# Attention and a routed expert layer on one core: a smaller first warming tile, and one store for both row halves at the end

## The chip, the cores and the metric

The kernel runs on one core of one Trainium2 chip. Its metric is the device time of one execution in microseconds; lower is better. The kernel before takes 374.43 us (median of three runs, 373.29 to 374.58). A profile of one execution, taken by the hardware, shows what each engine of the core did: TensorE (PE; its weight loads PEld), VectorE (DVE), ScalarE (ACT), GpSimd (POOL) and SyncE (SP), and the 16 DMA engines.

## The reference

The kernel computes grouped-query attention and then a two-level routed expert layer on its output. Cut to what matters:

```python
# q: (8, 16, 384, 64), k and v: (8, 4, 384, 64), all float32; four query heads share one k and v
scores = (1 / sqrt(64)) * q @ k.T
attn = softmax(scores)
x = (attn @ v).transpose(0, 2, 1, 3).reshape(8 * 384, 1024)

g_idx = argmax(x @ w_group)            # 4 groups, softmax weight g_w of the chosen one
e_idx = argmax(x_of_group @ w_expert)  # 4 experts in the group, softmax weight e_w
h = maximum(x_of_expert @ w1[g, e], 0)         # 1024 -> 1024
out[tokens] = g_w * e_w * (h @ w2[g, e])       # 1024 -> 1024, out: (3072, 1024) float32
```

The kernel works batch by batch. It guesses one expert for each batch of 384 tokens, computes that expert for all tokens of the batch, and weights the rows. What a guess leaves over is done in a loop at the end, which runs zero times for these inputs.

## The kernel before

Two places matter: the first eight microseconds and the last fifteen. `P` is 128, `S` 384, `SC` 3 (chunks of 128 tokens in a batch), `NC` 6, `DM` 1024, `HALF` 512, `FQ` 8, `B` 8.

At the start, TensorE multiplies a tile of ones, so that it is busy while the first keys and queries arrive:

```python
onesb = cpool.tile([P, 4 * P], BF16)
nc.vector.memset(onesb, 1.0)
nc.sync.dma_start(out=k0f[:, 0], in_=rows(k[0])[:, 0])
for m in range(KG):
    nc.scalar.dma_start(out=q0f[:, m], in_=rows(q[0])[:, m])
# ... (cut: the other loads; on ScalarE's queue also the gate weights, 8 and 32 rows)

def first_k(gp, which, eng):      # keys of the first two kv heads, transposed
    lo = gp * NC
    pt = ps_tile(which, [P, 16, P], BF16)
    for i in range(NC):
        for s in range(2):
            nc.tensor.transpose(out=pt[s * D:(s + 1) * D, i, :], in_=k16[0][:, lo + i],
                                identity=id128b)
    evac(eng, kT[0][:, lo:lo + NC, :], pt[:, :NC, :])   # copy to SBUF on eng

def first_scores():
    # ... (cut)
    def fill(n):                  # n warming products of 512 columns
        for i in range(n):
            nc.tensor.matmul(out=warm[:, i % 2, :], lhsT=onesb[:, :P], rhs=onesb, start=True,
                             stop=True)

    fill(8)
    nc.vector.tensor_copy(out=k16[0][:, :NC].rearrange("p c d -> p (c d)"), in_=k0f[:, 0])
    nc.scalar.copy(out=qraw[0][:, 0], in_=q0f[:, 0])
    nc.vector.tensor_copy(out=qraw[0][:, 1], in_=q0f[:, 1])
    first_k(0, "s", nc.vector)
    fill(2)
    first_q(0, SC, "s", nc.scalar)      # first query head pair, transposed, copied by ScalarE
    first_q(SC, SC, "o", nc.vector)     # second
    fill(2)
    return fill
# ... (cut) then the first two score tiles, and fill(4)
```

`k0f` and `q0f` are float32 as loaded; the three copies cast them to bfloat16.

At the end, the last batch's second product is done chunk by chunk, in halves of 512 columns. Each half is scaled by the row weight `w` on its way from PSUM to SBUF and stored at once. A chunk's 128 partitions are two groups of 64, which belong to different row sets of the output: row `6 * p + x` for partition `p` of the group, with `x` = 0 and 2 for chunk 0, 4 and 1 for chunk 1, 3 and 5 for chunk 2.

```python
def out_rows(o):
    return o.rearrange("(p x) d -> x p d", x=NC)

def halves(c):
    for h in range(2):
        j = 2 * c + h
        yield slice(h * H2, (h + 1) * H2), 2 * (j % SC) + j // SC

for c in range(SC):
    ot = opool.tile([P, DM], F32, name="ot")
    for nh in range(2):
        y = ps_tile("so"[nh])
        ffn_y(w2s[B - 1], hTs[B - 1], c, "", (nh,), y)      # eight products of 512 columns
        sl = slice(nh * HALF, (nh + 1) * HALF)
        w = weff[B - 1][:, c:c + 1]
        if (c, nh) == (SC - 1, 1):
            q1 = slice(HALF, HALF + HALF // 2)
            q2 = slice(HALF + HALF // 2, DM)
            nc.scalar.mul(ot[:, q1], y[:, nh, :HALF // 2], w)
            nc.vector.tensor_scalar(ot[:, q2], y[:, nh, HALF // 2:], w, None, op0=ALU.mult)
        elif nh:
            nc.vector.tensor_scalar(ot[:, sl], y[:, nh, :], w, None, op0=ALU.mult)
        else:
            nc.scalar.mul(ot[:, sl], y[:, nh, :], w)
        for i, (ps, x) in enumerate(halves(c)):
            eng = nc.scalar if (c, nh, i) == (SC - 1, 1, 1) else nc.sync
            eng.dma_start(out=out_rows(out[(B - 1) * S:])[x][:, sl], in_=ot[ps, sl])
```

Of the kernel before, what the change touches and what calls it, by code (L numbers as in the profile page):

```python
# [10 lines left out]
BF16 = mybir.dt.bfloat16  # L11
I32 = mybir.dt.int32
AX = mybir.AxisListType
ALU = mybir.AluOpType
# [4 lines left out]
def kernel(  # L19
# [11 lines left out]
    nc = tc.nc  # L31
    P = 128
    B, Hq, S, D = q.shape
    _, Hkv, _, _ = k.shape
    SC = S // P
    DM = Hq * D
# [5 lines left out]
    FQ = F // P  # L42
    NW = G + NE
    HALF = DM // 2
# [10 lines left out]
    cpool = ctx.enter_context(tc.tile_pool(name="const", bufs=1))  # L55
# [15 lines left out]
    def ps_tile(which, shape=None, dtype=F32):  # L71
        if which == "x":
            which = f"o{1 - turn['o']}"
        else:
            turn[which] = 1 - turn[which]
            which += str(turn[which])
        return psum.tile(shape or [P, 2, 512], dtype, name="ps_" + which)
# [6 lines left out]
    def rows(x):  # L84
        return x.rearrange("h (p c) d -> (h p) (c d)", c=NC).rearrange("(a p) n -> p a n", p=P)
# [19 lines left out]
    def new_qT(b):  # L105
        qT[b] = xpool.tile([P, KQ * SC, P], BF16, name="qT")

    def new_kT(b):
        kT[b] = xpool.tile([P, NK, P], BF16, name="kT")
# [36 lines left out]
                              in_=v[0, g0:g1].rearrange("h (p c) d -> p h (c d)", c=NC))  # L146

    onesb = cpool.tile([P, 4 * P], BF16)
    nc.vector.memset(onesb, 1.0)
    nc.sync.dma_start(out=k0f[:, 0], in_=rows(k[0])[:, 0])  # L150
    for m in range(KG):
# [10 lines left out]
    for g in range(1, Hkv):  # L162
        nc.gpsimd.dma_start(out=qraw[0][:, KG * g:KG * (g + 1)],
                            in_=rows(q[0])[:, KG * g:KG * (g + 1)])
# [73 lines left out]
    def evac(eng, out_, in_):  # L238
        if eng is nc.scalar:
            eng.copy(out=out_, in_=in_)  # L240
        else:
            eng.tensor_copy(out=out_, in_=in_)  # L242

    def first_k(gp, which, eng):
# [6 lines that stand above are left out]
        evac(eng, kT[0][:, lo:lo + NC, :], pt[:, :NC, :])  # L251

    def first_q(i0, n, which, eng):
        pt = ps_tile(which, [P, 16, P], BF16)
        for i in range(n):
            a, c = (i0 + i) // SC, (i0 + i) % SC
            nc.tensor.transpose(out=pt[:, i, :], in_=qraw[0][:, a, c * P:(c + 1) * P],
                                identity=id128b)
        evac(eng, qT[0][:, i0:i0 + n, :], pt[:, :n, :])

    def first_scores():
        new_kT(0)
        new_qT(0)
        warm = ps_tile("o")

        def fill(n):
            for i in range(n):
                nc.tensor.matmul(out=warm[:, i % 2, :], lhsT=onesb[:, :P], rhs=onesb, start=True,  # L268
                                 stop=True)

        fill(8)
        nc.vector.tensor_copy(out=k16[0][:, :NC].rearrange("p c d -> p (c d)"), in_=k0f[:, 0])
        nc.scalar.copy(out=qraw[0][:, 0], in_=q0f[:, 0])
        nc.vector.tensor_copy(out=qraw[0][:, 1], in_=q0f[:, 1])
        first_k(0, "s", nc.vector)
        fill(2)
        first_q(0, SC, "s", nc.scalar)
        first_q(SC, SC, "o", nc.vector)
        fill(2)
        return fill  # L280
# [263 lines left out]
    weff = {}  # L544
# [13 lines left out]
    ers, w1s, w2s = {}, {}, {}  # L558
# [39 lines left out]
# [8 lines that stand above are left out]
# [11 lines left out]
    def ffn_y(w2, hT, c, which, nhs=(0, 1), y=None, fs=None):  # L617
        if y is None:
            y = ps_tile(which)
        for nh in nhs:  # L620
            for f in (range(FQ) if fs is None else fs):
                nc.tensor.matmul(out=y[:, nh, :], lhsT=hT[:, f, c * P:(c + 1) * P],  # L622
                                 rhs=w2[:, f, nh * HALF:(nh + 1) * HALF],
                                 start=(f == 0), stop=(f == FQ - 1))
        return y
# [10 lines left out]
    hTs = {}  # L636
# [23 lines left out]

    gate_constants()
    fill = first_scores()
    index_constants()
    at = {0: Attn(0), 1: Attn(1)}
# [215 lines left out]

    for c in range(SC):
        ot = opool.tile([P, DM], F32, name="ot")
        for nh in range(2):
            y = ps_tile("so"[nh])
            ffn_y(w2s[B - 1], hTs[B - 1], c, "", (nh,), y)
            sl = slice(nh * HALF, (nh + 1) * HALF)
            w = weff[B - 1][:, c:c + 1]
            if (c, nh) == (SC - 1, 1):
                q1 = slice(HALF, HALF + HALF // 2)
                q2 = slice(HALF + HALF // 2, DM)  # L890
                nc.scalar.mul(ot[:, q1], y[:, nh, :HALF // 2], w)
                nc.vector.tensor_scalar(ot[:, q2], y[:, nh, HALF // 2:], w, None, op0=ALU.mult)
            elif nh:
                nc.vector.tensor_scalar(ot[:, sl], y[:, nh, :], w, None, op0=ALU.mult)
            else:
                nc.scalar.mul(ot[:, sl], y[:, nh, :], w)
            for i, (ps, x) in enumerate(halves(c)):
                eng = nc.scalar if (c, nh, i) == (SC - 1, 1, 1) else nc.sync
                eng.dma_start(out=out_rows(out[(B - 1) * S:])[x][:, sl], in_=ot[ps, sl])
    region.close()  # L900

    n_left = nc.values_load(left_i[0:1, 0:1], min_val=0, max_val=B * NE)
# [1 line left out]
    with tc.For_i(0, n_left, 1):  # L904
# [15 lines left out]
        x = xpool.tile([P, KQ, S], BF16, name="xb")  # L920
# [15 lines left out]
        for c in range(SC):  # L936
            ot = opool.tile([P, DM], F32, name="ot")
            for ps, x_ in halves(c):
                nc.sync.dma_start(out=ot[ps], in_=orows[x_])
            y = ffn_y(w2, hT, c, "s")  # L940
            nc.vector.scalar_tensor_tensor(ot, y.rearrange("p a n -> p (a n)"), we[:, c:c + 1],
                                           ot, op0=ALU.mult, op1=ALU.add)
# [32 lines left out]
```

The softmax here doesn't subtract the row's maximum and nothing guards it: scores larger than these inputs give would overflow.

## Time and profile before

| | before |
|---|---|
| time, median of three runs | 374.43 us |
| span of the profiled execution | 372.4 us |
| TensorE clock granted, mean | 0.994 |
| first warming product starts | 1.60 us |
| first key transposes start | 5.13 us |
| first scores start | 7.52 us |
| last output products start | 363.75 us |
| last stores are issued | 366.70 us |
| stores in the last chunks | 12 of 128 KB each |

The profile's times are microseconds from the start of the span. A line of the timeline has the start, the duration, the engine, the line of the kernel, the operation, the tiles (written <- read) and the number of instructions merged into it. What stands in brackets is the idle time of the engine just before, and what ended it. An engine's name with a `q` is its queue, which issues DMAs and waits; the duration of an issue is that of issuing and not of the transfer. The DMA view gives packets, megabytes and the time that the packets took as a share of 16 engines' time, by queue: q1 is SyncE's, q10 ScalarE's, q0 GpSimd's. Under its issues stand the size and the median time from issue to landing.

### The profile page before, as it was taken

The page shows a single profiled execution, that of the slowest core. Times are in us where ns is not written, and L with a number is a line of the kernel's source. Part 1 is how long each engine was busy: PE and PEld are TensorE (multiplying, and loading weights), DVE is VectorE, ACT ScalarE, POOL GpSimd, SP SyncE. Part 2 cuts the span into 40 slices and gives each one's busy share as a digit, 9 for nine tenths or more (in the row PEclk, how much of TensorE's full clock was granted, in tenths as well). Part 3 has the DMA queues.
Part 4 walks back from the last instruction along what each step waited for, and adds up shares of the span by engine and source line. Part 5 has one row for each costly group of instructions (what it writes and reads, how often), then busy time and mean ns, then how long its engine had stood idle before and what let it go on. Part 6 is the DMA issues. An engine that isn't in the chain of part 4 may idle for free.

```text
span 372.4 us, 8914 instructions
## 1 busy us (share of the span) xinstructions
PE 361.1 (97%) x3648; PEld 183.8 (49%) x3663; DVE 258.1 (69%) x491; ACT 233.0 (63%) x309; POOL 150.6 (40%) x118
## 2 busy tenths in 40 slices
PE   8999999999999999999999999999999999999992
PEld 3545446445454545544555445544545445554641
DVE  5699787858976498737989189764897379892230
ACT  4789943759926597367954599265972679544221
POOL 6666950706804176033730367113760237500000
PEclk9999999999999999999999999999999999999997
DMA  8986999999999999999999999989999999999734
GB/s 189 242 108 101 241 213 156 234 239 281 222 152 184 249 263 210 147 195 291 238 208 153 255 246 216 199 167 246 264 212 150 203 212 238 196 201 234 238 73 99
DMA packets 71209, 76.02 MB, mean 204 GB/s; under 512 B 35928, under 2 KB 50264, under 8 KB 71168
## 3 DMA queue, kind: packets, MB, share of 16 engines
q0 software_dynamic: 26640, 41.03, 63.0%
q1 hardware_dynamic: 44096, 33.81, 37.1%
q8 instruction: 29, 0.48, 0.5%
q10 hardware_dynamic: 432, 0.61, 0.5%
q14 instruction: 12, 0.10, 0.1%
HBM read 89.21 MB, written 18.87 MB: 290 GB/s over the span
## 4 chain that ended last, share of the span: by engine, by line
PE 91%; DVE 3%; ACT 2%; issue 1%; POOL 1%; ACTq 0%; POOLq 0%
PE ps_o L324 29%; PE ps_s L611 21%; PE ps_s L622 14%; PE ps_s L305 8%; PE ps_o L622 8%; PE ps_o L446 3%; PE ps_o L268 2%; DVE red L338 1%; PE ps_o L611 1%; PE ps_o L408 1%; ACT e L311 1%; PE ps_s L473 1%; DVE ps_o L419 1%; DVE xT L428 1%; POOL e L331 1%
## 5 line engine op out<-in xcount | busy, mean ns | idle before, releaser
L311 ACT ACTIVATE e<-ps_s 128x768 f32<-128x768 f32 x192 | 150.3, 814 | 22.1 <-PE ps_s L305 19.3
L324 PE MATMUL ps_o<-e,v_raw 64*64 64x384 f32 x1536 | 153.1, 482 | 0.2 <-DVE xT L428 0.2
L331 POOL TENSOR_TENSOR e<-e 128x768 f32<-128x768 f32 x64 | 116.1, 1832 | 88.6 <-ACT e L311 64.6
L338 DVE TRANSPOSE_TENSOR_REDUCE red<-e 128x24 f32<-128x768 f32 x128 | 114.3, 947 | 11.9 <-POOL e L331 11.9
L611 PE MATMUL ps_s<-xb,w 128*128 128x384 bf16 x480 | 81.1, 326 | 0.4 <-ACT hT L615 0.2
L324 PEld LDWEIGHTS ps_o<-e,v_raw 64*64 64x64 f32 x1536 | 55.4, 133 | 37.5 <-issue 27.1
L611 PEld LDWEIGHTS <-w 128*128 128x128 bf16 x512 | 48.9, 98 | 36.1 <-issue 3.9
L305 PE MATMUL ps_s<-qT,kT 64*64 64x384 bf16 x768 | 63.7, 326 | 0.4 <-ACT e L311 0.2
L615 ACT ACTIVATE hT<-ps_s 128x768 bf16<-128x768 f32 x30 | 24.3, 810 | 61.0 <-PE ps_s L611 61.0
L622 PEld LDWEIGHTS <-hT 128*128 128x128 bf16 x384 | 35.5, 98 | 45.1 <-issue 6.5
L622 PE MATMUL ps_s<-w,hT 128*128 128x512 bf16 x240 | 56.0, 379 | 0.4
L305 PEld LDWEIGHTS <-kT 64*64 64x64 bf16 x768 | 24.3, 105 | 38.4 <-issue 36.7
L678 POOL COPY after<-qT 128x1 bf16<-128x1 bf16 x7 | 2.1, 301 | 79.8 <-DMA qT<-q_raw 76.9
L622 PE MATMUL ps_o<-w,hT 128*128 128x512 bf16 x129 | 31.1, 379 | 0.6 <-issue 0.2
L419 DVE STREAM_TRANSPOSE rb<-inv 128x384 f32<-128x384 f32 x60 | 31.0, 555 | 0.3
L647 ACT ACTIVATE ot<-ps_s,we 128x1024 f32<-128x1024 f32 x14 | 15.6, 1114 | 19.1 <-PE ps_s L622 19.1
L428 DVE TENSOR_TENSOR xT<-xT,rb 128x768 f32<-128x768 f32 x25 | 24.0, 958 | 0.9
L242 DVE CAST vm<-ps_s 128x4 bf16<-128x4 f32 x5 | 0.8, 163 | 29.8 <-PE ps_s L460 29.8
L240 ACT CAST xb<-xT 128x768 bf16<-128x768 f32 x27 | 21.1, 827 | 0.0
L374 DVE COPY xT<-ps_o 128x768 f32<-128x768 f32 x18 | 16.5, 919 | 0.0
L376 ACT COPY xT<-ps_o 128x768 f32<-128x768 f32 x10 | 8.0, 801 | 6.5 <-PE ps_o L324 6.5
L242 DVE COPY gl<-ps_s 128x80 f32<-128x80 f32 (+1 forms) x6 | 1.4, 239 | 14.0 <-PE ps_s L478 8.4
(132 smaller groups left out, 196.8 us busy)
## 6 DMA issues: line engine op xcount, KB each, us to landing
w<-in_moe_w_dram POOLq DMA_DIRECT2D x16, 2048.0 KB, 21.8
out_dram<-ot SPq DMA_DIRECT2D x42, 256.0 KB, 7.1
xb_scratch<-xb SPq DMA_DIRECT2D x8, 768.0 KB, 9.6
q_raw<-in_q_dram POOLq DMA_DIRECT2D x7, 768.0 KB, 33.7
v_raw<-in_v_dram SPq DMA_DIRECT2D x14, 384.0 KB, 5.6
out_dram<-ot SPq DMA_DIRECT2D x11, 128.0 KB, 2.3
k<-in_k_dram POOLq DMA_DIRECT2D x7, 192.0 KB, 30.5
w<-in_q_dram POOLq DMA_DIRECT2D x3, 192.0 KB, 6.7
```

Source lines behind the costliest of these rows:

```text
L240: eng.copy(out=out_, in_=in_)
L305: nc.tensor.matmul(out=sT[r * H2:(r + 1) * H2, s, :S], lhsT=kT[b][s * D:(s + 1) * D, slot, ks], rhs=qT[b][s * D:(s + 1) * D, kq * SC:(kq + ...
L311: nc.scalar.activation(e.rearrange("p t (s x) -> p s t x", s=2), sT[:, :, :S].rearrange("p s (t x) -> p s t x", t=2), ACT.Exp, scale=scale)
L324: nc.tensor.matmul(out=oT[t * D:(t + 1) * D, r, :S], lhsT=vraw[b][r * H2:(r + 1) * H2, g, c * D:(c + 1) * D], rhs=self.e[u][r * H2:(r + 1) ...
L331: eng.tensor_add(out=self.e[u], in0=self.e[u], in1=self.e[u + 1])
L338: nc.vector.tensor_reduce(out=reds[self.b][:, g, n].rearrange("p t j -> p (t j)"), in_=self.e[u].rearrange("p t (j x) -> p (t j) x", x=32) ...
L374: nc.vector.tensor_copy(out=dst, in_=src)
L419: nc.vector.transpose(out=rb[:, r].rearrange("p (j x) -> p j x", x=32), in_=inv[b][:, 2 * m + r].unsqueeze(2).to_broadcast([P, NB, 32]))
L428: eng.tensor_mul(out=x, in0=x, in1=rb)
L611: nc.tensor.matmul(out=h[:, jj, :S], lhsT=w1[:, kq, (f0 + jj) * P:(f0 + jj + 1) * P], rhs=x[:, kq, :], start=(kq == 0), stop=(kq == KQ - 1))
L615: nc.scalar.activation(hT[:, f0:f0 + 2, :], h[:, :, :S], ACT.Relu)
L622: nc.tensor.matmul(out=y[:, nh, :], lhsT=hT[:, f, c * P:(c + 1) * P], rhs=w2[:, f, nh * HALF:(nh + 1) * HALF], start=(f == 0), stop=(f == ...
```

## The change

At the start, a tile of ones of 128 columns is set before the one of 512. Four small products on it begin the warming, and six large ones follow where there were eight. One of the two large products between the key and query transposes goes, and the other moves behind the first query transposes. The first key copy moves from VectorE to ScalarE, and the first query copy from ScalarE to VectorE. This is for an earlier start of TensorE, and for transposes that wait for fewer warming products.

At the end, the last chunk's output is made in three parts (512, 256 and 256 columns) with a PSUM tile of its own for each, where the last half was one tile read by two engines. Where the second row set has the larger index (chunks 0 and 2), one store takes all 128 partitions and both row sets; chunk 1 keeps two stores for each part. All stores go out on SyncE's queue. This is for fewer stores, and for a last part whose copy and store are short.

```diff
     onesb = cpool.tile([P, 4 * P], BF16)
+    ones1 = cpool.tile([P, P], BF16)
+    nc.vector.memset(ones1, 1.0)
     nc.vector.memset(onesb, 1.0)
@@ first_scores
-        fill(8)
+        for i in range(4):
+            nc.tensor.matmul(out=warm[:, i % 2, :P], lhsT=ones1, rhs=ones1, start=True, stop=True)
+        fill(6)
         # (cut: the three casts, unchanged)
-        first_k(0, "s", nc.vector)
-        fill(2)
-        first_q(0, SC, "s", nc.scalar)
+        first_k(0, "s", nc.scalar)
+        first_q(0, SC, "s", nc.vector)
+        fill(1)
         first_q(SC, SC, "o", nc.vector)
         fill(2)
@@ the last batch's output
-        for nh in range(2):
-            # (cut: the whole body, as printed above)
+        w = weff[B - 1][:, c:c + 1]
+        (ps0, x0), (ps1, x1) = halves(c)
+        parts = [(0, HALF), (HALF, DM)]
+        if c == SC - 1:
+            parts = [(0, HALF), (HALF, 3 * HALF // 2), (3 * HALF // 2, DM)]
+        for i, (n0, n1) in enumerate(parts):
+            y = ps_tile("so"[i % 2])
+            for f in range(FQ):
+                nc.tensor.matmul(out=y[:, 0, :n1 - n0], lhsT=hTs[B - 1][:, f, c * P:(c + 1) * P],
+                                 rhs=w2s[B - 1][:, f, n0:n1], start=(f == 0), stop=(f == FQ - 1))
+            if i % 2:
+                nc.vector.tensor_scalar(ot[:, n0:n1], y[:, 0, :n1 - n0], w, None, op0=ALU.mult)
+            else:
+                nc.scalar.mul(ot[:, n0:n1], y[:, 0, :n1 - n0], w)
+            rows_out = out_rows(out[(B - 1) * S:])
+            if x1 > x0:
+                nc.sync.dma_start(out=rows_out[x0:x1 + 1:x1 - x0, :, n0:n1],
+                                  in_=ot[:, n0:n1])
+            else:
+                for ps, x in ((ps0, x0), (ps1, x1)):
+                    nc.sync.dma_start(out=rows_out[x][:, n0:n1], in_=ot[ps, n0:n1])
```

More of the change, by code (lines that the diff above doesn't have):

```diff
@@ L882 @@
         ot = opool.tile([P, DM], F32, name="ot")
-        for nh in range(2):
[L884 to L894, printed above, removed]
-            else:
[L896 to L899, printed above, removed]
+        w = weff[B - 1][:, c:c + 1]
[10 more added lines that the diff above has]
+                nc.vector.tensor_scalar(ot[:, n0:n1], y[:, 0, :n1 - n0], w, None, op0=ALU.mult)
+            else:
+                nc.scalar.mul(ot[:, n0:n1], y[:, 0, :n1 - n0], w)
[6 more added lines that the diff above has]
+                    nc.sync.dma_start(out=rows_out[x][:, n0:n1], in_=ot[ps, n0:n1])
     region.close()
```

## The prediction

> **What bounds the kernel now.** I read the page first: the first table, then the row of forty slices.
>
> ```profile
> PE 361.1 (97%) x3648; PEld 183.8 (49%) x3663; DVE 258.1 (69%) x491; ACT 233.0 (63%) x309; POOL 150.6 (40%) x118
> ...
> PE   8999999999999999999999999999999999999992
> ```
>
> TensorE is busy in every slice but the last, so what is before the first product and after the last one is added to the whole. The change touches only these two ends. I therefore asked the timeline for the first 9.2 us and the last 9 us.
>
> At the start (columns: start us, duration us, engine, line, operation, tiles):
>
> ```profile
> 1.06 0.48 DVE L149 MEMSET onesb<- 128x512 bf16 x1 [1.06 <-PEq L959]
> 1.60 3.60 PE L268 MATMUL ps_o<-onesb 128*128 128x512 bf16 x8 [1.60 <-DVE onesb L149]
> 4.10 0.44 DVE L272 CAST w<-w 128x384 bf16<-128x384 f32 x1 [0.75 <-DMA w<-in_k_dram]
> 5.13 0.85 PE L249 MATMUL ps_s<-id128b,w 128*64 128x128 bf16 x12
> 5.17 0.68 DVE L274 CAST w<-w 128x384 bf16<-128x384 f32 x1 [0.63 <-DMA w<-in_q_dram]
> 5.91 0.87 PE L268 MATMUL ps_o<-onesb 128*128 128x512 bf16 x2
> 6.02 0.56 DVE L242 COPY kT<-ps_s 128x768 bf16<-128x768 bf16 x1 [0.18 <-PE ps_s L249]
> 7.16 0.36 DVE L242 COPY qT<-ps_o 128x384 bf16<-128x384 bf16 x1 [0.58 <-PE ps_o L257]
> 7.52 0.56 PE L305 MATMUL ps_s<-qT,kT 64*64 64x384 bf16 x8
> ```
>
> The keys are cast by 4.54 (4.10 + 0.44), but their transposes start at 5.13: TensorE is still in its eight warming products. The second query head is cast by 5.85 (5.17 + 0.68), but two more warming products stand ahead of the query transposes. The first scores start at 7.52.
>
> At the end:
>
> ```profile
> 363.75 1.89 PE L622 MATMUL ps_o<-w,hT 128*128 128x512 bf16 x8
> 365.68 0.47 ACT L891 ACTIVATE ot<-ps_o,we 128x256 f32<-128x256 f32 x1 [1.04 <-PE ps_o L622]
> 366.19 0.48 DVE L892 TENSOR_SCALAR ot<-ps_o,we 128x256 f32<-128x256 f32 x1 [3.21 <-ACT ot L891]
> 366.70 0.55 ACTq L899 DMA_DIRECT2D out_dram<-ot  x1
> ```
>
> The two quarter evictions run one after the other, and the last stores go out at 366.70. The DMA answer for 366 to 370 us has the queues (packets, MB, packet time as a share of 16 engines) and the stores:
>
> ```profile
> q1 hardware_dynamic: 213, 0.34, 39.4%
> q10 hardware_dynamic: 80, 0.13, 8.9%
> ...
> out_dram<-ot ACTq DMA_DIRECT2D x1, 128.0 KB, 3.0
> ```
>
> So the last landing is at 366.70 + 3.0 = 369.7, and the span ends 2.7 us later, at 372.4, after the closing waits. Until 369.7 the end is set by the stores. That is the number to keep: whatever moves the last landing moves the time.
>
> [...] Its page has:
>
> ```profile
> q10 hardware_dynamic: 432, 0.61, 0.5%
> ```
>
> ScalarE's queue issues five transfers: two of 128 rows, one of 8 (the group weights), one of 32, one of 64. That is 360 rows; if each is one packet, 72 packets are completions, which is 4 x 16 + 8. So the 8-row transfer used 8 engines[...].
>
> [...] In the DMA answer above q1 has 39.4% of 16 x 4.0 us = 25.2 us of packet time for 213 - 48 = 165 rows, 0.153 us for a row of 2 KB, where mostly one half store is in flight; q10, overlapping a store of the other half, has 8.9% = 5.7 us for 64 rows, 0.089 us.
>
> [...] the warming products' weight loads start at 2.01, 2.43, 2.86.
>
> **The front, part by part.** A memset of 128 bf16 columns precedes that of 512. I take 0.17 us for it, from the 128-column float memset in this trace. Then TensorE can start at 1.06 + 0.17 + 0.05 = 1.28 instead of 1.60. Four small products cost a quarter of 0.427 each, 0.43 us, to 1.71; onesb is ready at about 1.06 + 0.17 + 0.48 = 1.71 to 1.75. Six large products take 6 x 0.427 = 2.56, to 4.3. The key cast is bound by its load, so it still ends at 4.54. The transposes start at about 4.6 instead of 5.13: 0.5 us earlier, and end near 5.45.
>
> The key eviction moves to ScalarE, which is free from 4.95 (cast at 4.44, 0.51 us). I take 0.8 us, as for its other 768-column operations: 5.5 to 6.3, against 6.58 before. VectorE finishes the second head's cast at 5.85, evicts the first head (0.36) by 6.25. One warming product (0.43) and three transposes end about 6.45, the eviction takes 0.36, to 6.9. The two later warming products end about then too. Scores at 6.9 to 7.0 instead of 7.52: a gain of 0.55 us. TensorE then stays the bound, and no DMA wait of hundreds of ns stands between; I let all 0.55 carry to the end.
>
> **The tail on TensorE and the evictions.** The last half becomes two products of 256 columns per step, 8 + 8, of half the time each: the last ends where it did,[...]. The two quarter evictions no longer wait for one another: VectorE's is done during the last products, ScalarE's ends at 365.68 + 0.47 = 366.15. The last store goes out near 366.2, 0.5 us earlier.
>
> **The tail's stores.** Twelve half stores become nine: two merged of 256 KB (chunk 0), four half stores (chunk 1, where the second row index is smaller), three merged (chunk 2: 256, 128 and 128 KB). The merged store's DRAM pattern is [2 row sets, 64 rows, columns], its slowest dimension is 2; SBUF's is 128. [...] Each of two engines then carries 64 rows, serially. From the packet times above, one engine's work:
> - chunk 0: 2 x 64 x 0.088 = 11.3 us
> - chunk 1: 4 stores x 4 rows x 0.153 = 2.4 us
> - chunk 2: 64 x 0.088 = 5.6, and 2 x 64 rows of 1 KB. I take 0.048 for these, an estimate between half of 0.088 and all of it: 6.1 us
>
> The sum is 25.4 us. The first data now move 1.1 to 1.3 us after the first issue at 358.23, about 359.4; shifted by 0.55, 358.9. All later stores are issued before 367, while the two engines still work on chunk 0, so they never starve: the end is 358.9 + 25.4 = 384.3, plus 0.3 for the completion, 384.6. Against 369.7 that is +14.9. The front's gain is already in the start. So 374.43 + 14.9 = 389.3; I say 389.
>
> **The rivals.**
> 1. All 16 engines take the merged store (the pattern is rearranged on its way to the hardware, or the split runs over all 128 rows). Then the tail gains: issue 0.5 us earlier, landing near 2.0 us after it instead of 3.0, [...] (0.089 against 0.153 a row). That is -1.5, with the front's -0.55: 372.4. [...] Against: the 8-row load kept to 8 engines. I give it 0.19.
> 2. Two engines, but at the crowded 0.153 us a row: chunk 0 becomes 19.6, chunk 2 about 20; the end about 401 and the time near 407. Against: [...] nothing else moves data then.
> 3. Two engines faster than 0.088,[...]: at 0.075 a row, the time is near 386.
> 4. The front gives its gain back: ScalarE's slower key eviction, or a colder clock at the scores. Worth at most 0.5 us either way, lost beside the stores.
>
> **Range and chances.** I put 0.8 on two engines (centre 389, 384 to 396 mostly) and 0.19 on sixteen (371.8 to 373). A range from 372 to 395 holds both. Two per cent is 7.5 us: two engines pass it, sixteen can't reach it downwards. Faster 0.01, same 0.19, slower 0.80.
>
> **What would show it.** First scores near 6.9 instead of 7.52; key transposes near 4.6. Merged 256 KB stores that land 6 us after issue for the first and over 12 for the later ones, instead of 2.3. The slices after the last product at one or two tenths of DMA busy (2 of 16 engines), some 45 GB/s instead of 200. Fewer completions on the SP queue. The span's end 2.7 us after the last landing. If the merged store lands in 2 to 2.5 us, k was 16 and I am wrong by 17 us; if the landing is late but the rate is 25 GB/s, rival 2 is right.

## The result and the profile after

The changed kernel takes 388.09 us (median of four runs, 387.61 to 388.92) against 373.99 for the kernel before, measured beside it: a ratio of 1.038, 95% interval 1.0349 to 1.0411. It is slower by some 14 us; 389 was predicted.

The row of forty slices of the changed kernel's page, whose slices are 9.7 us long (PE's busy tenths, then the mean busy tenths of the 16 DMA engines and the GB/s that they moved):

```profile
PE   8999989999999999999999999999999999999800
...
DMA  8976999999999999999998999899999999993310
GB/s 196 232 107 112 239 209 135 257 275 256 207 146 206 299 225 155 189 259 258 209 150 188 285 224 206 163 256 253 211 150 215 228 227 178 209 273 105 82 52 31
```

TensorE is as dense as before, but its last two slices are empty: it has finished, and the core waits for about 21 us. In the same slices the DMA engines are at one tenth and under one tenth. They are the last thing to work, and nearly all of them are idle. The DMA view of the stretch from 370 to 384 us shows how many work:

```profile
DMA  1111111101111111111111111111111111111000
...
DMA packets 457, 0.64 MB, mean 46 GB/s; under 512 B 16, under 2 KB 272, under 8 KB 457
...
q1 hardware_dynamic: 457, 0.64, 12.6%
```

12.6% of 16 engines is 2.0 engines, for 14 us on end. A later piece, 379 to 382 us, has rows of 1 KB alone:

```profile
DMA packets 144, 0.15 MB, mean 48 GB/s; under 512 B 2, under 2 KB 144, under 8 KB 144
...
q1 hardware_dynamic: 144, 0.15, 13.6%
```

13.6% of 16 x 3 us is 6.5 us of packet time for 142 rows: 0.046 us a row of 1 KB. In the trace, the packets of 2 KB rows that the merged stores write take 0.084 us. The evictions are not late, as the timeline of the end shows:

```profile
365.49 9.98 SPq L903 DMA_DIRECT2D out_dram<-ot  x3
365.78 0.47 ACT L900 ACTIVATE ot<-ps_s,we 128x256 f32<-128x256 f32 x1 [1.06 <-PE ps_s L895]
```

The last eviction ends at 366.25, 0.4 us before the 366.67 of before. But SyncE needs 9.98 us to issue its last three stores. The answer for the output tile has the durations of the issues one by one (min/median/max in ns; L903 are the merged stores, L907 the half stores of chunk 1), and the time to landing of those whose landing could be told:

```profile
L903 SPq DMA_DIRECT2D out_dram<-ot x5: 526/642/5138, 358.3 to 370.3; - x5
...
L907 SPq DMA_DIRECT2D out_dram<-ot x4: 541/826/1667, 361.3 to 364.8; - x4
...
DMA to landing us min/median/max: 8.1/8.7/10.4
```

In the kernel before, the same answer has:

```profile
L899 SPq DMA_DIRECT2D out_dram<-ot x11: 466/478/594, 358.2 to 366.7; - x11
...
DMA to landing us min/median/max: 2.2/2.3/3.0
```

The half stores of chunk 1 are of the old kind, which landed in 2.3 us there. Here they take 8.1 to 10.4: part of their rows seem to stand behind chunk 0's merged stores in the queues of the two engines, which `merged_first_chunk` tests below. The landings of the merged stores themselves can't be told from the profile.

At the start (the same lines as before, of the changed kernel):

```profile
1.20 0.61 PE L274 MATMUL ps_o<-ones 128*128 128x128 bf16 x4 [1.20 <-DVE ones L150]
...
4.50 0.45 DVE L276 CAST w<-w 128x384 bf16<-128x384 f32 x1 [1.15 <-DMA w<-in_k_dram]
...
5.00 0.85 PE L251 MATMUL ps_s<-id128b,w 128*64 128x128 bf16 x12 [0.52 <-DVE w L276]
...
7.07 0.60 PE L309 MATMUL ps_s<-qT,kT 64*64 64x384 bf16 x8
```

TensorE starts 0.4 us earlier, and now waits 0.52 us for the keys: their load, and not the warming, is the bound. The first scores are 0.45 us earlier. Yet the first product of the closing chunks is at 355.20, where it was at 355.12. In this execution that gain is gone again, and where it went is a question for the experiments.

### The profile page after: what moved, and what is told of

Its sections match the earlier page's. It is cut to its first block, busy times and chain, and to the rows that moved or that the text cites. A ratio compares the mean times of both kernels' runs of the same rounds, so it can differ in the third digit from the quotient of the medians.

```text
span 386.9 us, 8931 instructions
## 1 busy us (share of the span) xinstructions
PE 360.6 (93%) x3657; PEld 184.7 (48%) x3672; DVE 257.9 (67%) x492; ACT 233.2 (60%) x309; POOL 150.7 (39%) x118
## 3 DMA queue, kind: packets, MB, share of 16 engines
q1 hardware_dynamic: 44186, 33.94, 35.2%
## 4 chain that ended last, share of the span: by engine, by line
PE 84%; DVE 6%; ACT 2%; issue 1%; DMA 1%; POOL 1%; POOLq 0%; ACTq 0%
PE ps_o L328 26%; PE ps_s L615 21%; PE ps_s L626 13%; PE ps_s L309 7%; PE ps_o L626 6%; PE ps_o L450 3%; DVE red L342 2%; PE ps_s L895 2%; PE ps_o L615 1%; PE ps_o L895 1%; DMA w<-in_k_dram 1%; ACT e L315 1%; PE ps_s L477 1%; PE ps_o L412 1%; DVE xT L432 1%
## 5 line engine op out<-in xcount | busy, mean ns | idle before, releaser
L626 PE MATMUL ps_s<-w,hT 128*128 128x512 bf16 x217 | 50.3, 379 | 0.4
L626 PEld LDWEIGHTS <-hT 128*128 128x128 bf16 x336 | 30.8, 98 | 39.5 <-issue 6.5
L626 PE MATMUL ps_o<-w,hT 128*128 128x512 bf16 x105 | 25.5, 379 | 0.6 <-issue 0.2
```

## The experiments

Two theories stood against one another. **Theory:** the DRAM side of the merged store, [2 row sets, 64 rows, columns], has 2 as its slowest dimension, so two DMA engines carry it, row by row; the front's share is a few tenths. **Rivals:** a store of 128 partitions is slow in itself; or three parts and one issuing queue cost the time; or part of the loss comes from the front. Times are medians; a ratio is against runs of the kernel before on the same chip, with its 95% interval.

**One half of the change at a time.** `tail_only` is the kernel before with the new output loop; `front_only` is the kernel before with the new front:

```diff
 # front_only, against the kernel before
+    ones1 = cpool.tile([P, P], BF16)
+    nc.vector.memset(ones1, 1.0)
-        fill(8)
+        for i in range(4):
+            nc.tensor.matmul(out=warm[:, i % 2, :P], lhsT=ones1, rhs=ones1, start=True, stop=True)
+        fill(6)
-        first_k(0, "s", nc.vector)
-        fill(2)
-        first_q(0, SC, "s", nc.scalar)
+        first_k(0, "s", nc.scalar)
+        first_q(0, SC, "s", nc.vector)
+        fill(1)
```

> The kernel before with the new tail alone. If the tail's stores are the whole loss: 388.0 (+-0.7), as the changed kernel. If part of the loss came from the front (a colder clock, the evictions that changed engines): under 387.

Measured: 388.32 us, ratio 1.0386 (1.0364 to 1.0408), against 1.038 for the whole change. The tail is the whole loss.

> The kernel before with the new front alone. Reading of the changed kernel's trace: its first scores are 0.45 us earlier, but from 38 us on every product is 0.08 later, because GpSimd's one-element copy, which stands ahead of the first expert weights' load, waited until 30.80 us for one straggling DMA engine of the last query transpose, beside an instruction fetch that moved earlier with everything else. If that happens in each execution, the time is that of before, +0.1 (+-0.15). Rival: the straggler was this one execution's, and the gain carries as I predicted: -0.45 against before. Neither reaches 2%.

Measured: 373.78 against 373.83, ratio 0.9999 (0.9989 to 1.0009), so -0.04 us, between -0.4 and +0.35. The profile of this run doesn't show what the changed kernel's did. This is GpSimd's copy ahead of the load of the first expert weights, first in the changed kernel, then in `front_only`, as their waits on GpSimd list it (who waited for whom, us in total, times, longest):

```profile
POOL after L682 <- DMA qT<-q_raw: 3.4, 1, 3.4
```

```profile
POOL after L682 <- DVE red L342: 2.9, 1, 2.9
```

In the changed kernel the copy waited for the landing of the last query transpose, whose semaphore has fifteen of its sixteen updates by 29.99 us and the last at 30.80, and ran at 30.85; in `front_only` it waited for the choice of the expert and ran at 29.85. There the gain of the first scores (0.91 us in that execution) was still 0.88 at the first expert products. So the late transpose is something of single executions and not of the front: my first reading, that it happens each time, fell. One more profile with the new front has this wait, `two_queues`, and nine don't.

**The merged store undone.** `half_stores` is the changed kernel with two stores of 64 rows for each part:

```diff
-            if x1 > x0:
-                nc.sync.dma_start(out=rows_out[x0:x1 + 1:x1 - x0, :, n0:n1],
-                                  in_=ot[:, n0:n1])
-            else:
-                for ps, x in ((ps0, x0), (ps1, x1)):
-                    nc.sync.dma_start(out=rows_out[x][:, n0:n1], in_=ot[ps, n0:n1])
+            for ps, x in ((ps0, x0), (ps1, x1)):
+                nc.sync.dma_start(out=rows_out[x][:, n0:n1], in_=ot[ps, n0:n1])
```

> The changed kernel, but each part of chunks 0 and 2 is stored by two half stores of 64 rows on SyncE's queue, as chunk 1's are; parts, products and evictions are the change's. If the slowest dimension of size 2 confines the merged store to two engines, this takes all of the loss away: last store issued near 366.7 (two issues of 0.5 us after the eviction at 366.2), landing 2.3 later near 369.0 against 369.7 before: -0.7 against before, and up to -0.45 more if the front's gain carries. Rival: the three parts, or all stores on one queue, cost the time: then it stays above 380.

Measured: 374.14 us, ratio 1.0001 (0.9991 to 1.0012). The 14 us are gone: as their cause, the rival of the three parts and the one queue falls. But the 0.7 us that I expected beside it didn't come. Its timeline shows why:

```profile
362.20 5.62 SPq L903 DMA_DIRECT2D out_dram<-ot  x8
...
364.90 0.47 ACT L900 ACTIVATE ot<-ps_s,we 128x256 f32<-128x256 f32 x1 [1.06 <-PE ps_s L895]
```

The last eviction is done at 365.37, but SyncE issues eight stores without a break until 367.82, 0.70 us each on average. It has a backlog, and the last part waits in it: its two stores leave at 366.64 and 367.24.

**The slowest dimension, set by hand.** These four change nothing on the SBUF side. Every part of all three chunks is one store of 128 partitions, into a block of 128 neighbouring rows, which is seen in four ways. The output's rows are placed differently from the reference's, so these times are for the reading of the store and not for use; chunk 1 is merged here too.

```diff
-            if x1 > x0:
-                # (cut: the merged store and the two half stores)
+            blk = out[(B - 1) * S + c * P:(B - 1) * S + (c + 1) * P]
+            nc.sync.dma_start(out=blk.rearrange("(p a) d -> a p d", a=2)[:, :, n0:n1],   # or 4, 8
+                              in_=ot[:, n0:n1])
+            # outer128: out=blk[:, n0:n1]
```

> The changed kernel, but every part of all three chunks is one 128-partition store, into a block of 128 neighbouring rows seen as [2, 64, columns] with the outer step of one row. The output rows are placed differently from the reference's; bytes, row lengths and the SBUF side are the same. [...] two engines; one engine's work is 6 x 64 rows of 2 KB less the last, i.e. 5 x 64 x 0.084 + 2 x 64 x 0.046 = 32.8 us from about 359.5, last landing 392.6, span 395.3, time near 396.5. Rival (128-partition stores are slow whatever the pattern): the same as outer128.

> As outer2, but the block is seen as [4, 32, columns]. [...] four engines. If each keeps 0.084 us a row: 16.4 us of work from 359.5, landing 376.2, time near 380. [...] (0.153 us a row of 2 KB, 0.08 of 1 KB): 24.5 + 5.1 = 29.6 us, time near 393. Rival: as outer128.

> As outer2, but the block is seen as [8, 16, columns]. [...] eight engines. Uncrowded, 8.2 us of work: less than the 6.6 us over which the parts come out plus the first wait, so the landing is bound by the last parts, near 369.5, time near 374. Crowded, 14.8 us: landing near 374.5, time near 379. Rival: as outer128.

> As outer2, but the block is seen as it lies, [128, columns]: the slowest dimension is 128 on both sides. [...] sixteen engines, the store lands about 2.1 us after its issue near 366.2, at 368.3, 1.4 earlier than before: time 372.5 to 373. Rival (a store of 128 partitions and 256 KB is itself slow): above 380.

The DMA views of `outer2` (368 to 388 us), `outer4` (368 to 376), `outer8` (362 to 368) and `outer128` (364.5 to 367.5), in this order:

```profile
DMA packets 560, 1.02 MB, mean 51 GB/s; under 512 B 8, under 2 KB 120, under 8 KB 560
...
q1 hardware_dynamic: 560, 1.02, 13.2%
```

```profile
DMA packets 513, 0.80 MB, mean 100 GB/s; under 512 B 16, under 2 KB 225, under 8 KB 513
...
q1 hardware_dynamic: 513, 0.80, 26.5%
```

```profile
DMA packets 458, 0.88 MB, mean 146 GB/s; under 512 B 26, under 2 KB 34, under 8 KB 458
...
q1 hardware_dynamic: 458, 0.88, 48.1%
```

```profile
DMA  0789999899999996200002799972000000000000
GB/s 0 273 328 410 437 355 382 300 382 355 342 342 341 328 382 232 55 0 0 0 0 96 273 328 382 341 246 82 0 0 0 0 0 0 0 0 0 0 0 0
```

The pages of the four runs, in the same order, count the packets on SyncE's queue over the whole kernel:

```profile
q1 hardware_dynamic: 44126, 33.94, 34.5%
q1 hardware_dynamic: 44140, 33.94, 36.3%
q1 hardware_dynamic: 44168, 33.94, 37.4%
q1 hardware_dynamic: 44224, 33.94, 36.9%
```

| slowest dimension in DRAM | busy engines (share x 16) | GB/s | time us | ratio, interval |
|---|---|---|---|---|
| 2 | 2.1 | 51 | 395.97 | 1.058, 1.0504 to 1.0656 |
| 4 | 4.2 | 100 | 381.49 | 1.0193, 1.0122 to 1.0264 |
| 8 | 7.7 | 146 | 374.87 | 1.0023, 1.0014 to 1.0032 |
| 128 | nearly 16 in bursts | 300 to 437 in bursts | 371.53 | 0.993, 0.9917 to 0.9942 |

The same bytes, row lengths and partitions: only the number in front of the DRAM pattern differs, and with it the step between one engine's rows, and the busy engines follow it. The packet counts go with it exactly. The rows are the same in all four, so what differs is the completions, which the trace has as packets of 4 bytes. After 357 us there are 14, 28, 56 and 112 of them; for seven stores that is 2, 4, 8 and 16 for each, close to the busy engines in the table (2.1, 4.2, 7.7 and nearly 16). The changed kernel fits too: its page has 44186 packets on this queue and that of `half_stores` 44336; the 150 between them are the completions of ten half stores, sixteen each, less those of five merged ones, two each. For these stores that is the theory shown. The rival of the slow 128-partition store falls with `outer128`, the fastest of all.

The time of `outer2` came within 0.6 us of its sum (its profiled span, 393.8, was 1.5 us under it), that of `outer8` within 0.9, that of `outer4` within 1.5 of the one at 0.084 us a row; the 0.153 us was wrong for it. `outer128` was 1 us faster than expected. In its profile the last store is issued at 365.3 and not near 366.2, so most of that comes ahead of the store; its stores land in 1.9 to 2.4 us.

**How long the two engines hold others up.** `merged_first_chunk` merges chunk 0's stores alone and has half stores on two queues elsewhere (as `two_queues`, below):

```diff
+            if c == 0:
+                nc.sync.dma_start(out=rows_out[x0:x1 + 1:x1 - x0, :, n0:n1],
+                                  in_=ot[:, n0:n1])
+                continue
```

> two_queues, but chunk 0's two stores are merged as in the change; they leave 7 us before the last ones. If a later store's rows wait behind them on the same two engines: 10.75 us of chunk 0 from about 359.2, then those engines' share of chunks 1 and 2 (16 + 8 rows of 2 KB, 16 of 1 KB, about 3 us), last landing near 373, time near 377. Rival: stores don't wait for one another, only chunk 0's own 5.4 us a store counts, ending near 370: no more than 1.5 us over two_queues.

Measured: 378.65 us, ratio 1.0122 (1.0106 to 1.0138), 1.7 above the sum. Its DMA view of the end gives the stores by issuing queue:

```profile
out_dram<-ot SPq DMA_DIRECT2D x4, 128.0 KB, 8.9
out_dram<-ot ACTq DMA_DIRECT2D x2, 128.0 KB, 4.9
```

Two merged stores 7 us ahead of the end still cost about 5 us against `two_queues`. On SyncE's own queue the half stores wait behind them, 8.9 us to landing; on ScalarE's they pass some of it, 4.9 us. That the sum was short by 1.7 fits SyncE's timeline, where the last two issues begin only after 371 us; I didn't take that stall apart.

**Towards a version that keeps the gain.** Three runs take issues away from SyncE. `half_stores_2q` moves one, the last; `two_queues` moves the second half store of each part that ScalarE evicts; `fewer_stores` also stores the last chunk's first 768 columns together:

```diff
 # two_queues, against half_stores
-            for ps, x in ((ps0, x0), (ps1, x1)):
-                nc.sync.dma_start(out=rows_out[x][:, n0:n1], in_=ot[ps, n0:n1])
+            for h, (ps, x) in enumerate(((ps0, x0), (ps1, x1))):
+                eng = nc.scalar if h and i % 2 == 0 else nc.sync
+                eng.dma_start(out=rows_out[x][:, n0:n1], in_=ot[ps, n0:n1])
 # fewer_stores, against two_queues
+            if c == SC - 1 and i == 0:
+                continue
+            m0 = 0 if c == SC - 1 and i == 1 else n0
-                eng = nc.scalar if h and i % 2 == 0 else nc.sync
-                eng.dma_start(out=rows_out[x][:, n0:n1], in_=ot[ps, n0:n1])
+                eng = nc.scalar if h and (i % 2 == 0 or c == SC - 1) else nc.sync
+                eng.dma_start(out=rows_out[x][:, m0:n1], in_=ot[ps, m0:n1])
```

> The same, but the second half store of the very last part goes out on ScalarE's queue, so the last two stores are issued together near 366.2. If the last landing alone sets the end: another 0.5 us earlier than half_stores, -1.2 against before. Rival: ScalarE's own closing chain, which in the kernel before ran 2.6 us from its store's issue to its last wait (366.70 to 369.31), takes over: then no more than 0.1 us better than half_stores, or worse.

> The changed kernel with half stores of 64 rows everywhere, where of each part that ScalarE evicts the second half store goes out on ScalarE's queue: ten issues on SyncE, four on ScalarE. In the run with all fourteen on SyncE the last eviction was done at 365.37 and its stores left at 366.64 and 367.24, since SyncE issues one every 0.6 to 0.7 us. If that backlog is what ate the tail's gain: last issue near 365.9, landing near 368.1, 1.2 us less than half_stores, 372.6 to 373.0. Rival: ScalarE's closing chain sets the end, or its issues (0.55 us each) delay its evictions: within 0.4 of half_stores.

> two_queues, but the last chunk's first two parts (768 columns) are stored together, and of each of its two pairs the second half goes out on ScalarE's queue: twelve stores, eight on SyncE. In two_queues SyncE issued its last three at 365.46, 366.10 and 366.79, though the last eviction was done at 366.05: it was still working off a backlog. If SyncE's cadence of 0.6 us an issue sets the end of the tail: its last issue comes right after the eviction, 0.6 us earlier, time 372.7 against 373.3. Rival: with ScalarE's chain, or the 3 KB rows' longer transfer, at the end: within 0.3 of two_queues.

Measured: 373.40 (ratio 0.9985, 0.9977 to 0.9993), 373.28 (0.9975, 0.9959 to 0.9991) and 372.80 (0.9961, 0.9947 to 0.9974). The first is 0.7 us under `half_stores`, the second 0.9 where 1.2 was expected; in both SyncE still issues last, near 367. In the third it doesn't:

```profile
364.48 0.49 ACTq L907 DMA_DIRECT2D out_dram<-ot  x1
365.02 0.47 ACT L900 ACTIVATE ot<-ps_s,we 128x256 f32<-128x256 f32 x1 [1.28 <-PEq L912]
365.52 0.50 ACTq L907 DMA_DIRECT2D out_dram<-ot  x1
```

The last store leaves 0.03 us after the eviction. This version beats both kernels, the one before by 0.4%. Its 0.5 us over `two_queues` is as expected, but the intervals of the two overlap, so this step alone is not shown.

`two_queues_old_front` puts the tail of `two_queues` on the front of before:

> The same tail on the front of the kernel before; the pair measures the front once more. If the front is worth the 0.45 us that its profiles show: 0.45 slower than two_queues. If it is worth nothing, as the front alone measured (interval -0.4 to +0.35 us): the same within 0.3.

Measured: 374.41 us, ratio 1.0004 (0.9993 to 1.0016). So here the front is worth 1.1 us, roughly 0.3 to 1.8. The two measurements of the front agree only near -0.35 to -0.4. It also means that neither the new front alone (0.9999) nor this tail alone (1.0004) is shown to gain anything; only both together are (0.9975). Why is open.

## Why the prediction was right, and where it was not

| step | predicted | in the profile after |
|---|---|---|
| first warming product | 1.28 | 1.20 |
| key transposes | 4.6 | 5.00 |
| first scores | 6.9 to 7.0 | 7.07 |
| last eviction done | 366.15 | 366.25 |
| engines of a merged store | 2 | 2.0 |
| row of 2 KB | 0.088 us | 0.084 us |
| row of 1 KB | 0.048 us | 0.046 us |
| first data of the stores | 358.9 | 359.6 |
| two engines' work, first data to last | 25.4 us | 24.2 us |
| last data | 384.3 | 383.8 |
| last completion after the last data | 0.3 us | 0.33 us |
| from the last data to the end of the span | 3.0 us | 3.1 us |

**The tail** was right in mechanism and close in size. Part of the closeness is luck: the two engines' work was put 1.2 us too long and its start 0.7 us too early, and the two errors partly cancel. The evidence for two engines was also thin. Of the 432 packets on ScalarE's queue of the kernel before 72 have 4 bytes, so the 8-row load gave away eight completions instead of sixteen. But eight rows can't occupy more than eight engines however they are shared out, so it could not tell a split over the slowest dimension from the rival of a split over all rows. The step to two engines for a slowest dimension of 2 (the prediction's k is the number of engines) was an assumption that no trace of before shows; the runs here show it, with 2.1, 4.2, 7.7 and nearly 16 busy engines for slowest dimensions of 2, 4, 8 and 128.

The rival of sixteen engines (372.4) is near what `outer128` shows, 371.53, where chunk 1 is merged too: had the pattern been of that kind, the change would probably have paid. The rival of crowded rows (407) fell: the rows took 0.084 us, not 0.153. The rival of faster rows (386) had the right direction, but 0.075 was too fast.

**The statement that all later stores are issued before 367** was wrong. SyncE's last issue began at 370.3 and took 5.14 us. It cost nothing, since the two engines never ran dry: from 360 to 382.7 us the trace has at least two packets in flight at all but 0.04 us. The sum of their work set the end in either case.

**The front** can't be judged by the changed kernel's profile alone. There the step "I let all 0.55 carry to the end" failed: its scores were 0.45 earlier, its later products 0.08 later. Its key transposes came late too, at 5.00, because the keys did (cast from 4.50). In the ten other profiles with the new front the cast starts at 3.98 to 4.29 and the transposes at 4.42 to 4.70, as predicted. Over all eleven the first scores come at 6.6 to 7.4, over the three with the old front at 7.1 to 7.6; the means are 0.6 us apart, and those of the first closing product still 0.5.

Much of the spread goes with the moment from which the trace records the full TensorE clock, anywhere from 4.1 to 7.3 us. The two warming products just ahead of the scores show what that does: they take 0.59 us in `front_only`, which has the full clock from 5.2, and 1.03 us in `outer4`, which has it from 7.3. The large warming products at the very start, ahead of that moment in the kernel before and in the changed one, cost what was predicted, 0.427 us each: in both their weight loads start 0.42 to 0.43 us apart.

Two pairs of profiles have nearly the same moment and different fronts. `tail_only` (old front, 5.64) has its first scores at 7.15 and `outer128` (new, 5.57) at 6.59; `two_queues_old_front` (6.75) has them at 7.64 and `two_queues` (6.74) at 7.11. Both times the new front is 0.5 to 0.6 us earlier, as predicted. The times of many runs are less clear: -0.04 in one measurement, which reaches to -0.4 at most, and -1.1 in another. How much of the 0.55 arrives at the end is open. Why the last query transpose lands late in some executions is open too. In both where GpSimd's copy waited for it, the late completion coincides with an instruction fetch through the core's DMA engines (a packet from 29.57 to 31.0 us in the changed kernel, from 29.35 to 30.5 in `two_queues`); no run was made to show it as the cause.

**The earlier last store** (0.5 us, near 366.2) needs a SyncE that can issue at once, as in `outer128`, where the last of seven stores leaves 0.03 us after its eviction. In the changed kernel it left at 370.3, 4.1 us after. The same parts as half stores, which the prediction had not priced, are fourteen: at 0.6 to 0.7 us an issue SyncE itself became the bound, as `half_stores` showed.

## What to carry to other kernels

Before two stores are merged, write down both access patterns and look at the number in front. In these stores it decided how many DMA engines worked, and a merged store of twice the bytes on an eighth of the engines was far slower than two (388 us against 374). The later stores waited too: in `merged_first_chunk` two merged stores early in the tail still cost about 5 us at the end. And near the end of a kernel count the issues of one queue as work: here they took 0.5 to 0.7 us each, and in `half_stores` the last part's first store waited 1.27 us for its issuer (366.64, its data ready at 365.37).

## What was not expected of the hardware

- The issue of a store itself took microseconds here. With the merged stores on two engines, SyncE's issues grew from 0.5 us to 4.10 and 5.14 us in the changed kernel; the longest took 2.35 us with four engines (`outer4`), 0.87 with eight and 0.34 with sixteen.
- Rows took no longer with four engines than with two: `outer4` moved 100 GB/s at 26.5% of packet time, 0.084 us a row of 2 KB, just as two engines do, while the half stores of the kernel before took 0.153. `outer128` is at 0.084 to 0.089 with sixteen engines. Why the rows of a half store took longer is not settled.
- The same front, run again, gives first scores at 6.6 to 7.4 us, and the full clock is granted anywhere from 4.1 to 7.3 us. A change of 0.4 us at a kernel's start is not read from one profile of each.
